# Chunked attention before a mixture of experts: 64x64 tiles of the array in place of zero blocks, and transposes moved further ahead

## The chip, the cores and the metric

The kernel runs on one core of a Trainium2 chip. The metric is the device time of one execution in microseconds (us); of the kernel before three executions were timed, with a median of 689.94 us (687.65 to 695.09). The engines are called as in the profile: PE is TensorE's matmul side and PEld its weight loads, DVE is VectorE, ACT is ScalarE, POOL is GpSimd, SP is SyncE, which here only issues DMAs.

## What is computed

Attention within chunks of 64 tokens (8 batches, 8 heads, 576 tokens, head size 64), then a mixture of 16 experts in 4 groups of 4, one expert for each of the 4608 tokens. Cut to what matters:

```python
scores = q_c @ k_c.T / 8            # a chunk of 64 tokens against itself, for each head
attn = exp(scores - max(scores))
attn = attn / (sum(attn) + 1e-9)
x = (attn @ v_c)                    # then 4608 tokens of 512 numbers
g = argmax(x @ w_group); e = argmax(x @ w_expert[g])
out = gate(g) * gate(e) * (relu(x @ w1[g, e]) @ w2[g, e])
```

All of the attention is in float32.

## The kernel before

Tokens are worked on in 36 tiles of 128 tokens, two chunks each. A tile goes through these steps, each a function with a letter, by which the order is written:

- `load_qk(u)` (Q, line 248) brings q and k of two tiles; a partition holds two neighbouring tokens of all heads. `load_v(t)` (V, line 257) brings v of a tile in four DMAs of 64 KB. Both go through SP's queue, in the order of the program. q and k have three buffers, v has `NV = 4`.
- `stage_a(t)` (a, lines 271 and 274): eight transposes on PE, into two banks of the pool `ps_t`, and four copies of 64 partitions by DVE and ACT. They give q^T and k^T for half of the heads of two tiles. k^T goes into a buffer (`kz`) in which the other head of a pair has a block of zeros.
- `stage_b(t)` (b, line 288): scores. Eight matmuls; each contracts over 128 rows (two heads) for one chunk, with 64 columns of q^T as weights and 128 columns of k^T and zeros moving. The profile has two records for each float32 matmul, so 16.
- `stage_sub` (s, lines 296 and 299, DVE), `stage_exp` (e, line 305, ACT): row maximum, difference, exponential.
- `stage_ct(t)` (c, lines 311 and 313): four transposes of the probabilities on PE, one copy by ACT.
- `stage_pv(t)` (p, line 327): weighted sums, eight matmuls of 130 columns (two heads of 64 and a column of ones, with blocks of zeros in `va`).
- `stage_norm(t)` (n, lines 341 to 352, DVE): division by the sum that the column of ones gives.
- `stage_xt(t)` (x, lines 364 and 365): four transposes for the router, one copy by ACT.

After each four tiles the router runs: logits (line 371, four matmuls of 32 columns of weights and 512 moving columns, in the four column strips of the array), a transpose back (line 384), a chain of small DVE operations (`route`, spread between others by `more`), ranks, and four indirect DMAs by POOL that put the tokens in the order of their experts.

The order on PE, DVE and ACT is written by hand: a string `HEAD` for the first tiles, a loop for tiles 8 to 34, a string `TAIL` for the end. In the loop, at step t, PE does a(t), then b(t-2), x(t-5), c(t-3), p(t-4). The first expert's weights are loaded by POOL (F0, F1, F4, F5 in `EXTRA`) and split in two parts (P0 to P7) while the attention runs. Then a loop over the experts' tokens follows, which the change leaves as it was.

Of the kernel before, what the change touches and what calls it, by code (L numbers as in the profile page):

```python
# [42 lines left out]
EXTRA = {26: "F0", 28: "F1", 29: "F2 F3 P0", 30: "P1 P2", 31: "P3", 32: "P4 P5 F4", 33: "P6 X0", 34: "P7 X1 F5"}  # L43
HEAD = ("V0 a0 Q2 a1 b0 V1 s0 a2 e0 Q3 a3 V2 b1 s1 e1 c0 a4 b2 s2 V3 c1 Q4 e2 p0 n0 a5 b3 s3 e3 V4 a6 p1 V5"
        " n1 b4 s4 c2 a7 c3 p2 n2 x0 G0 e4 b5 x1 s5 Z0 p3 e5 x2 V6 c4 Z1 Q5 n3")
TAIL = ("c32 m1 b33 m1 36 m1 s33 p31 b34 e33 V35 W1 m4 x30 m1 n31 m3 s34 m1 L0 m1 e34 L1 c33 x31 b35 17 m2"
# [14 lines left out]
def constants():  # L61
# [9 lines left out]
    # the first unit stands in the row behind the experts and goes before them  # L71
# [18 lines left out]
def moe_kernel(tc, q, k, v, w_group, w_expert, w1, w2, cst, out):  # L90
# [3 lines left out]
    with ExitStack() as ctx:  # L94
        dpool = ctx.enter_context(tc.tile_pool(name="dram", bufs=1, space=DRAM))
        wpool = ctx.enter_context(tc.tile_pool(name="wts", bufs=1))
        # the tokens of each expert in order: x, the token's number, its gate weight
# [7 lines left out]
        # rows that stand behind an expert's tokens: zeros with an out-of-range token  # L105
# [9 lines left out]
        # of the first unit: its tokens' rows, its expert, what it takes off each expert  # L115
# [23 lines left out]
        # a bank of the router's, then of the first layer's  # L139
# [14 lines left out]
        # the first unit's weights are brought in, and its w1 split, while the attention runs  # L154
        alloc_w(wpool, 0, 0, 2)

        def late2(i):
            if i not in wt[0]:
                pool, tag = ((kpool, "kz"), (vpool, "va"))[i > 3]
                m, c, n = W_PARTS[i]  # L160
                wt[0][i] = pool.tile([P, c, n], F32R, name=m + "0", tag=tag)
            return wt[0][i]
# [23 lines left out]
        def prep_static(i):  # L186
            # the first half of the columns, then the second
            i = i % 4 * 2 + i // 4
            h, l, r = (z.rearrange("p a b -> p (a b)") for z in (wt[0][0], wt[0][1], w1r[i // 4]))
            w, o = i * 512, i % 4 * 512  # L190
            nc.scalar.copy(h[:, w:w + 512], r[:, o:o + 512])
            nc.gpsimd.tensor_sub(l[:, w:w + 512], r[:, o:o + 512], h[:, w:w + 512].bitcast(F32))

        with ExitStack() as c1:
# [6 lines left out]
            ps_t = c1.enter_context(tc.tile_pool(name="pst", bufs=4, space=PSUM))  # L201
# [11 lines left out]
            # zeros where one head's part would meet the other's  # L213
            vbufs, kbufs = [], []
            for i in range(2):
                kz = kpool.tile([P, 4, 2, 2 * P], F32, name="kz%d" % i, tag="kz")
                for x in range(2):
                    (nc.gpsimd if x else nc.vector).memset(kz[64 * x:64 * x + 64, :, 1 - x, :], 0.0)
                kbufs.append(kz)
            for i in range(NV):  # L220
                va = vpool.tile([P, 2, 4, 2, HD + 1], F32, name="va%d" % i, tag="va")
                for x in range(2):
                    nc.gpsimd.memset(va[64 * x:64 * x + 64, :, :, 1 - x, :], 0.0)
                    nc.gpsimd.memset(va[64 * x:64 * x + 64, :, :, x, HD:HD + 1], 1.0)
# [13 lines left out]
            def load_qk(u):  # L238
                # a partition holds two neighbouring tokens of each head
                s = st["u", u] = {}  # L240
                both = lpool.tile([P, 2, H, P], F32, name="qk", tag="big")
                for x, nm in enumerate("qk"):
                    s[nm + "s"] = both[:, x]
                for hh in range(2) if u == 0 else (slice(None),):
                    hs = hh if u else slice(hh, H, 2)
                    for x, src in enumerate((q, k)):
                        for i, m, b, j in spans(4 * u, 4):
                            nc.sync.dma_start(
                                both[i * 32:(i + m) * 32, x, hs],
                                src[b, hs, j * CH:(j + m) * CH, :].rearrange("h (r a) d -> r h (a d)", a=2))  # L250

            def load_v(t):
                va = vbufs[t % NV]
                for c in range(2):
                    b, j = divmod(2 * t + c, NCH)
                    for x in range(2):
                        nc.sync.dma_start(
                            va[64 * x:64 * x + 64, c, :, x, 0:HD],
# [3 lines left out]
            def stage_a(t):  # L262
                u, hh = divmod(t, 2)
                s = st["u", u]
                if hh == 0:
                    s["qT"] = apool.tile([P, 4, 2 * P], F32, name="qT")
                r = slice(64 * hh, 64 * hh + 64)
                for nm, dst, eng in (("qs", s["qT"][r], nc.vector.tensor_copy if t < 2 else nc.scalar.copy), ("ks", kbufs[u % 2][r, :, hh, :], nc.vector.tensor_copy)):
                    pt = ps_t.tile([P, 4, P], F32, name="tp")
                    for i in range(4):  # L270
# [1111 lines left out]
```

## Time and profile before

| | us |
|---|---|
| median of three executions | 689.94 |
| lowest, highest | 687.65, 695.09 |
| profiled execution, span from first to last instruction | 700.9 |
| attention, to the scores of tile 32 | about 0 to 189 |
| end of the attention and the tables of the experts | about 190 to 250 |
| experts | about 250 to 688 |

The profiled execution is given by its span alone; that span is 11 us above the median of the timed ones. The page shows which engine is busy when; the chain of waits goes back from the last instruction to what each step waited for; the view of stretches gives busy time, granted clock (PEclk, 1.00 is full) and the share of the 16 DMA engines.

### The profile page before, as it was taken

To read this page: it belongs to the slowest core of one execution; us is meant where nothing else is said; L and a number is where in the kernel's file an instruction comes from. 1 tells how busy PE (TensorE), PEld (TensorE's weight loads), DVE (VectorE), ACT (ScalarE), POOL (GpSimd) and SP (SyncE) were. 2 spreads that over 40 slices of the span, in tenths; PEclk is the share of its full clock that TensorE was granted. 3 is DMA by queue.
4 is the path that set the end of the run, shared out by engine and by line. 5 is a ranking of instruction groups with operands and counts; after the bars stand their busy time and mean duration, and the time that the engine had idled before them with its cause. 6 is when DMAs were issued, how large, how long until landed. Compare 5 with 4: busy or idle time off the path is not lost.

```text
span 700.9 us, 14708 instructions
## 1 busy us (share of the span) xinstructions
PE 635.7 (91%) x4714; PEld 549.8 (78%) x4715; DVE 398.5 (57%) x738; ACT 324.1 (46%) x452; POOL 169.3 (24%) x272
## 2 busy tenths in 40 slices
PE   5989999879787879999998799999999999999991
PEld 4867777657566778898987789898999988898980
DVE  5766778747648656722649475572731868753220
ACT  5766777658544243511536355151511474551110
POOL 4002220227225222112226221222111214312110
PEclk9999999999898989999999899999999999999996
DMA  9988989999662596831357775645441757831100
GB/s 219 187 188 207 229 183 210 263 218 302 135 195 92 158 340 227 311 117 47 110 198 250 260 263 188 214 167 170 159 148 60 266 212 241 327 110 57 30 30 15
DMA packets 115946, 127.97 MB, mean 183 GB/s; under 512 B 46462, under 2 KB 83582, under 8 KB 115904
## 3 DMA queue, kind: packets, MB, share of 16 engines
q1 hardware_dynamic: 105040, 93.77, 47.2%
q0 software_dynamic: 10864, 33.64, 14.2%
q8 instruction: 26, 0.43, 0.3%
q14 instruction: 16, 0.13, 0.1%
HBM read 106.23 MB, written 21.93 MB: 183 GB/s over the span
## 4 chain that ended last, share of the span: by engine, by line
PE 75%; DMA 13%; DVE 4%; issue 3%; SPq 1%; POOL 1%; ACT 0%; another core or an unknown queue 0%; POOLq 0%; DVEq 0%; ACTq 0%
PE py L836 25%; PE ph L821 16%; DMA qk<-in_k_dram 6%; PE lgk L821 5%; PE sc L288 3%; PE o L327 3%; PE tp L271 3%; PE ph L805 3%; PE tp L364 2%; DMA xgr<-xs 2%; DMA va<-in_v_dram 2%; PE tp L311 2%; PE py L853 2%; PE pxt L721 2%; DMA out_dram<-xl,io__3010 1%
## 5 line engine op out<-in xcount | busy, mean ns | idle before, releaser
L821 PE MATMUL ph<-xt,w1h 128*128 128x256 f32 x672 | 100.3, 286 | 6.3 <-issue 6.3
L976 ACT ACTIVATE hth<-ph 128x512 fp32r<-128x512 f32 x43 | 25.7, 597 | 156.5 <-PE ph L821 124.5
L821 PEld LDWEIGHTS ph<-xt,w1h 128*128 128x128 f32 x672 | 90.8, 195 | 7.8 <-issue 6.7
L1300 POOL DMA_INDIRECT out_dram<-xl,io__3010 x37 | 44.1, 1191 | 151.6 <-DVE xl L1037 143.8
L1051 DVE TENSOR_TENSOR w2l<-w2r,w2h 128x1024 fp32r<-128x1024 f32 x60 | 69.5, 1219 | 8.5 <-ACT w2h L991 5.1
L1047 DVE TENSOR_TENSOR w1l<-w1r,w1h 128x2048 fp32r<-128x2048 f32 x28 | 63.0, 2288 | 12.7 <-ACT w1h L963 11.0
L836 PE MATMUL py<-w2h,hth 128*128 128x512 f32 x264 | 69.0, 404 | 0.0
L836 PE MATMUL py<-w2l,hth 128*128 128x512 f32 x264 | 65.8, 391 | 0.0
L836 PE MATMUL py<-w2h,htl 128*128 128x512 f32 x264 | 65.5, 390 | 0.0
L1037 DVE TENSOR_SCALAR xl<-py,io__3010 128x512 f32<-128x512 f32 x33 | 24.7, 748 | 69.2 <-PE py L836 69.2
L1070 DVE SCALAR_TENSOR_TENSOR htl<-ph,hth 128x512 fp32r<-128x512 f32 x40 | 27.4, 688 | 60.7 <-ACT hth L976 58.4
L271 PE MATMUL tp<-cs,qk 128*128 128x128 f32 x288 | 42.6, 292 | 18.8 <-DMA qk<-in_q_dram 11.7
L836 PEld LDWEIGHTS py<-w2l,hth 128*128 128x128 f32 x264 | 49.5, 188 | 10.9
L836 PEld LDWEIGHTS py<-w2h,htl 128*128 128x128 f32 x264 | 49.6, 188 | 10.8
L836 PEld LDWEIGHTS py<-w2h,hth 128*128 128x128 f32 x264 | 48.8, 192 | 10.4 <-ACT hth L1022 0.7
L271 PEld LDWEIGHTS tp<-cs,qk 128*128 128x128 f32 x288 | 33.0, 148 | 30.2 <-issue 15.6
L821 PE MATMUL ph<-xt,w1l 128*128 128x256 f32 x336 | 55.1, 287 | 0.5 <-DVE w1l L1047 0.5
L963 ACT CAST w1h<-w1r 128x2048 fp32r<-128x2048 f32 x28 | 52.1, 1902 | 4.1 <-DMA w1r<-in_moe_w_dram 2.4
L967 ACT CAST w2h<-w2r 128x2048 fp32r<-128x2048 f32 x28 | 52.3, 1925 | 0.0
L274 ACT COPY qT<-tp 64x512 f32<-64x512 f32 x70 | 44.0, 629 | 16.2 <-PE tp L271 9.4
L499 POOL DMA_INDIRECT xs<-x,pos x24 | 23.8, 990 | 100.7 <-DVE xl L352 51.0
L821 PEld LDWEIGHTS ph<-xt,w1l 128*128 128x128 f32 x336 | 47.2, 195 | 0.7 <-DVE w1l L1047 0.7
(278 smaller groups left out, 1111.8 us busy)
## 6 DMA issues: line engine op xcount, KB each, us to landing
w1r<-in_moe_w_dram SPq DMA_DIRECT2D x30, 1024.0 KB, 5.9
w2r<-in_moe_w_dram SPq DMA_DIRECT2D x30, 1024.0 KB
xgr<-xs POOLq DMA_DIRECT2D x38, 257.0 KB, 5.3
va<-in_v_dram SPq DMA_DIRECT2D x144, 64.0 KB
qk<-in_q_dram SPq DMA_DIRECT2D x11, 512.0 KB
qk<-in_k_dram SPq DMA_DIRECT2D x11, 512.0 KB
w1r<-in_moe_w_dram POOLq DMA_DIRECT2D x2, 1024.0 KB
w2r<-in_moe_w_dram POOLq DMA_DIRECT2D x2, 1024.0 KB
```

The source lines that it names most:

```text
L271: nc.tensor.transpose(pt[:, i, :], s[nm][:, 2 * i + hh, :], ident)
L274: (nc.scalar.copy if x else eng)(tv[:, :, :, x], pt[64 * x:64 * x + 64])
L821: m = pe.matmul(ph[f // 2][:, f % 2 * 256:f % 2 * 256 + 256], w_[:, c, f * P:(f + 1) * P], a_[:, c, :], start=(i == 0), stop=(i == 11))
L836: m = pe.matmul(py[j], a_[:, f, half[j]], w_(b, f), start=(i == 0), stop=(i == 23))
L963: lambda b, s, j: ac.copy(wt[b][0][:, s], w1r[j]), K1)
L967: lambda b, s, j: ac.copy(wt[b][2 + j], w2r[j]), K2)
L976: ac.activation(hth()[:, 2 * b:2 * b + 2, :], ph[b].rearrange("p (f t) -> p f t", f=2), AF.Relu).then_inc(S["Ha"], 1)
L1037: return ve.tensor_scalar(out=yb[:, j, :], in0=py[j], scalar1=io_[:, j, 1:2], scalar2=None, op0=ALU.mult)
L1047: lambda b, s, j: ve.tensor_sub(wt[b][1][:, s], w1r[j], wt[b][0][:, s].bitcast(F32)), K1, js)
L1051: m = ve.tensor_sub(wt[b][4 + 2 * j + i], w2r[j][:, 2 * i:2 * i + 2], wt[b][2 + j][:, 2 * i:2 * i + 2].bitcast(F32))
L1070: ve.scalar_tensor_tensor(out=htl()[:, 2 * b:2 * b + 2, :], in0=ph[b].rearrange("p (f t) -> p f t", f=2), scalar=0.0, in1=hth()[:, 2 * b:2 ...
L1300: gp.indirect_dma_start(out, bass.IndirectOffsetOnAxis(ap=io[:, j, 0:1].bitcast(I32), axis=0), yb[:, j, :], None, bounds_check=N - 1, oob_ ...
```

## The change

The blocks of zeros go. Each head's scores and weighted sums contract over 64 rows only, so a matmul takes a 64x64 quarter of the array; there are 16 instead of 8 in each of b and p, with half the moving columns. `sc` grows to two banks (heads in the upper and the lower rows have a bank each), so `ps_t` falls from four banks to three. q^T and k^T now hold four tiles, in four buffers; `va` has five buffers instead of four and no zeros. `stage_a(n)` is cut in two: n counts q and k apart, four transposes each. The loop is rewritten: at step t it does b(t), p(t-2), a(2t+6), c(t-1), a(2t+7), x(t-3), so q and k are transposed three tiles ahead of their scores. q and k are loaded as soon as one of their three buffers is free, and the first two tiles' q and k are loaded by tile instead of by head parity.

```diff
-NV = 4
+NV = 5
-        kpool = ctx.enter_context(tc.tile_pool(name="kz", bufs=2))
-        vpool = ctx.enter_context(tc.tile_pool(name="va", bufs=NV))
+        kpool = ctx.enter_context(tc.tile_pool(name="qkT", bufs=4))
...
-            ps_t = c1.enter_context(tc.tile_pool(name="pst", bufs=4, space=PSUM))
+            ps_t = c1.enter_context(tc.tile_pool(name="pst", bufs=3, space=PSUM))
...
+            def stage_a(n):
+                u, i = divmod(n, 8)
+                if i < 2:
+                    st["T", u, i] = kpool.tile([P, 4, 512], F32, name="kT" if i else "qT", tag="qkT")
+                dst = st["T", u, i % 2]
+                pt = ps_t.tile([P, 4, P], F32, name="tp")
+                z, x = i % 2, i // 2 % 2
...
+                for hp in range(4):
+                    nc.tensor.transpose(pt[:, hp, :], st["q", n // 4][:, z, 2 * hp + x], ident)
...
+                for a in range(2):
+                    (nc.vector.tensor_copy if z and not a else nc.scalar.copy)(to[:, a], pt[64 * a:64 * a + 64])
...
+            TILES = [(x, c, slice(64 * x, 64 * x + 64), slice(64 * c, 64 * c + 64)) for x in range(2) for c in range(2)]
             def stage_b(t):
+                sc = ps_s.tile([P, 2, 512], F32, name="sc")
                 for hp in range(4):
-                    for c in range(2):
-                        k0 = P * (t % 2) + c * CH
-                        nc.tensor.matmul(sc[c * 64:c * 64 + 64, 2 * hp:2 * hp + 2, :], lhsT=st["u", u]["qT"][:, hp, k0:k0 + CH],
-                                         rhs=kbufs[u % 2][:, hp, :, k0:k0 + CH], start=True, stop=True)
+                    for x, c, rows, cols in TILES:
+                        k0 = c0 + c * CH
+                        nc.tensor.matmul(sc[cols, x, hp * CH:hp * CH + CH], lhsT=st["T", u, 0][rows, hp, k0:k0 + CH],
+                                         rhs=st["T", u, 1][rows, hp, k0:k0 + CH], start=True, stop=True)
...
             def stage_pv(t):
-                if t in (TL - 2, TL):
-                    o = [ps_s.tile([P, 512], F32, name="sc"), bank(True, "o")]
-                else:
-                    o = ps_s.tile([P, 2, 512], F32, name="o")
+                o = ps_s.tile([P, 2, 512], F32, name="o")
                 for hp in range(4):
-                    for c in range(2):
-                        nc.tensor.matmul(o[hp // 2][c * 64:c * 64 + 64, hp % 2 * 2 * W:hp % 2 * 2 * W + 2 * W],
-                                         lhsT=pT[:, hp, c * 64:c * 64 + 64],
-                                         rhs=s["va"][:, c, hp].rearrange("p h e -> p (h e)"), start=True, stop=True)
+                    for x, c, rows, cols in TILES:
+                        nc.tensor.matmul(o[cols, x, hp * W:hp * W + W], lhsT=pT[rows, hp, cols], rhs=s["va"][rows, c, hp], start=True, stop=True)
...
-                for t in range(8, TL):
-                    stage_a(t)
-                    if t % 2 == 1 and t // 2 + 2 < NT // 2:
-                        load_qk(t // 2 + 2)
...
-                    run("b%d s%d x%d c%d e%d" % (t - 2, t - 2, t - 5, t - 3, t - 2))
-                    run("p%d n%d" % (t - 4, t - 4))
-                    load_v(t - 1)
...
+                for t in range(TL - 2):
+                    run("b%d s%d p%d n%d" % (t, t, t - 2, t - 2))
...
+                    run("a%d" % (2 * t + 6) if t else FIRST)
...
+                    run("c%d e%d" % (t - 1, t))
+                    run("a%d" % (2 * t + 7))
+                    if t % 2 == 0 and t <= 26:
+                        run("Q%d" % (t // 2 + 4))
+                    run("x%d" % (t - 3))
+                    load_v(t + 2)
```

The order on PE in one tile of the loop before (tp are the banks of the transposes; qk, pr and x are what is transposed):

```order
L271 MATMUL tp<-cs,qk 128x128 x8
L288 MATMUL sc<-kz_130,qT 64x128 x8
L364 MATMUL tp<-cs,x 128x128 x4
L311 MATMUL tp<-cs,pr 128x128 x4
L327 MATMUL o<-va_151,pT 64x130 x8
```

The same in the kernel after:

```order
L298 MATMUL sc<-kT,qT 64x64 x16
L335 MATMUL o<-va_133,pT 64x65 x16
L279 MATMUL tp<-cs,qk 128x128 x4
L323 MATMUL tp<-cs,pr 128x128 x4
L279 MATMUL tp<-cs,qk 128x128 x4
L363 MATMUL tp<-cs,x 128x128 x4
```

Scores and weighted sums now stand side by side, and the sixteen transposes of a tile behind them; before, the two stood apart, with transposes between.

The first DMAs on SP's queue before (cs are constants, qk are q and k, va is v):

```order
L101 DMA cs<-in_cst_dram 128x128
L248 DMA qk<-in_q_dram 128x4x128
L248 DMA qk<-in_k_dram 128x4x128
L248 DMA qk<-in_q_dram 128x4x128
L248 DMA qk<-in_k_dram 128x4x128
L248 DMA qk<-in_q_dram 128x8x128
L248 DMA qk<-in_k_dram 128x8x128
L626 DMA cs<-in_cst_dram 128x349
L257 DMA va_136<-in_v_dram 64x4x64 x4
```

And after, from the second q of the first pair of tiles:

```order
L249 DMA qk<-in_q_dram 128x4x64
L249 DMA qk<-in_k_dram 128x4x64
L249 DMA qk<-in_q_dram 128x8x128
L249 DMA qk<-in_k_dram 128x8x128
L249 DMA qk<-in_q_dram 32x8x128
L249 DMA qk<-in_q_dram 96x8x128
L249 DMA qk<-in_k_dram 32x8x128
L249 DMA qk<-in_k_dram 96x8x128
L258 DMA va_127<-in_v_dram 64x4x64 x4
```

q and k of three pairs of tiles stand ahead of the first v, where two pairs stood.

## Rows read from the trace of the kernel before

**Rows 1.** Stretches: us; busy us of PE, PEld, DVE, ACT, POOL; PEclk, DMA share, GB/s.

```profile
0.00:190.00 190.00, 160.50 (x1687) 127.27 (x1688) 127.76 (x367) 128.49 (x227) 46.98 (x73) 0.96 0.95 215
190.00:250.00 60.00, 47.18 (x376) 38.87 (x377) 38.80 (x118) 22.86 (x36) 21.48 (x22) 0.89 0.49 161
250.00:690.00 440.00, 428.07 (x2655) 383.63 (x2654) 231.97 (x253) 172.72 (x191) 100.83 (x178) 0.98 0.51 176
```

**Rows 2.** Chain of waits, its longest DMA pieces: start us, us, what.

```profile
40.05 8.02 DMA qk<-in_k_dram
...
86.87 10.19 DMA qk<-in_k_dram
...
158.80 6.15 DMA va<-in_v_dram
164.96 16.32 DMA qk<-in_k_dram
```

**Rows 3.** Timeline of PE, 112 to 124 us: start us, us, engine, line.

```profile
112.16 1.11 PE L327 MATMUL o<-va,pT 128*64 128x130 f32 x16
113.21 1.09 PE L271 MATMUL tp<-cs,qk 128*128 128x128 f32 x8
114.23 1.09 PE L288 MATMUL sc<-kz,qT 128*64 128x128 f32 x16
115.25 0.66 PE L364 MATMUL tp<-cs,x 128*128 128x128 f32 x4
115.75 0.60 PE L311 MATMUL tp<-cs,pr 128*128 128x128 f32 x4
116.28 1.11 PE L327 MATMUL o<-va,pT 128*64 128x130 f32 x16
...
121.59 1.07 PE L371 MATMUL lgk<-xT,wg 128*32 128x512 f32 x8
122.59 1.09 PE L271 MATMUL tp<-cs,qk 128*128 128x128 f32 x8
123.52 0.60 PE L384 MATMUL lgk<-cs,lts 128*128 128x128 f32 x4
```

**Rows 4.** Timeline, the first and a late stage b, and SP's last v.

```profile
10.18 1.09 PE L288 MATMUL sc<-kz,qT 128*64 128x128 f32 x16 [1.48 <-ACT kz L274]
...
169.25 24.57 SPq L257 DMA_DIRECT2D va<-in_v_dram  x24
...
188.89 1.09 PE L288 MATMUL sc<-kz,qT 128*64 128x128 f32 x16
```

**Rows 5.** SP's issues of one line: ns minimum/median/maximum, first and last start.

```profile
L257 SPq DMA_DIRECT2D va<-in_v_dram x144: 595/615/6269, 7.6 to 193.2; - x144
...
L248 SPq DMA_DIRECT2D qk<-in_q_dram x25: 341/602/3091, 1.4 to 164.1; - x25
L248 SPq DMA_DIRECT2D qk<-in_k_dram x25: 312/633/4194, 1.8 to 165.0; - x25
```

**Rows 6.** What SP's queue waited for: us in total, times, longest us.

```profile
SPq L257 <- PE tp L271: 14.5, 9, 5.9
...
SPq L257 <- PE o L327: 5.9, 9, 1.7
SPq L257 <- PE tp L311: 5.3, 8, 1.7
```

**Rows 7.** Stretches of 5 us, columns as in rows 1.

```profile
75.00:80.00 5.00, 5.00 (x62) 4.25 (x59) 4.08 (x10) 4.30 (x8) 0.00 (x0) 1.00 0.56 116
...
165.00:170.00 5.00, 4.95 (x57) 3.52 (x56) 4.40 (x10) 4.89 (x10) 3.03 (x4) 1.00 1.13 277
```

**Rows 8.** Timeline of the end: weighted sums and divisions of tiles 33 and 34.

```profile
205.15 0.61 PE L327 MATMUL tp<-va,pT 128*64 128x130 f32 x8
206.28 1.11 PE L327 MATMUL o<-va,pT 128*64 128x130 f32 x16
206.88 0.41 DVE L352 TENSOR_TENSOR xl<-tp,rc 128x256 f32<-128x256 f32 x1
```

More of the change, by code (lines that the diff above doesn't have):

```diff
@@ L158, in late2 @@
             if i not in wt[0]:
-                pool, tag = ((kpool, "kz"), (vpool, "va"))[i > 3]
                 m, c, n = W_PARTS[i]
-                wt[0][i] = pool.tile([P, c, n], F32R, name=m + "0", tag=tag)
+                if i < 4:
+                    wt[0][i] = kpool.tile([P, c, n], F32R, name=m + "0", tag="qkT")
+                else:
+                    j = i - i % 2
+                    both = kpool.tile([P, 2 * c, n], F32R, name=m + "0", tag="qkT")
+                    wt[0][j], wt[0][j + 1] = both[:, 0:c], both[:, c:2 * c]
             return wt[0][i]
@@ L212, in moe_kernel @@
             nc.vector.memset(wg, 0.0)
[L214 to L219, printed above, removed]
+            vbufs = []
             for i in range(NV):
[L221 to L224, printed above, removed]
+                va = cpool.tile([P, 2, 4, HD + 1], F32, name="va%d" % i)
+                (nc.gpsimd if i else nc.vector).memset(va[:, :, :, HD:HD + 1], 1.0)
                 vbufs.append(va)
@@ L257, in load_v @@
                         nc.sync.dma_start(
-                            va[64 * x:64 * x + 64, c, :, x, 0:HD],
+                            va[64 * x:64 * x + 64, c, :, 0:HD],
                             v[b].rearrange("(hp h2) s d -> h2 s hp d", h2=2)[x, j * CH:(j + 1) * CH])
                 st[t] = dict(va=va)
[L262 to L270, printed above, removed]
-                        nc.tensor.transpose(pt[:, i, :], s[nm][:, 2 * i + hh, :], ident)
-                    tv = dst.rearrange("p h (r a) -> p h r a", a=2)
-                    for x in range(2):
-                        (nc.scalar.copy if x else eng)(tv[:, :, :, x], pt[64 * x:64 * x + 64])
@@ L282, in stage_b, with bank @@
+            def bank(end):
+                return ps_t.tile([P, 4, P], F32, name="tp").rearrange("p a b -> p (a b)") if end else lgk
+            TILES = [(x, c, slice(64 * x, 64 * x + 64), slice(64 * c, 64 * c + 64)) for x in range(2) for c in range(2)]
             def stage_b(t):
-                s, u = st[t], t // 2
-                sc = bank(t >= TL - 1, "sc").rearrange("p (h k) -> p h k", h=8)
+                s, u, c0 = st[t], t // 4, t % 4 * P
+                sc = ps_s.tile([P, 2, 512], F32, name="sc")
@@ L292, in stage_sub @@
+                s["sc"] = sc[:, :, 0:4 * CH].rearrange("p x (h k) -> p x h k", h=4)
             def stage_sub(t):
@@ L349, in stage_norm @@
                 x = st["x", g][:, i, 0:D]
-                xv = x.rearrange("p (a b d) -> p a b d", a=2, d=HD)
-                for z, r, y in zip(ov, rv, [xv[:, 0], xv[:, 1]] if two else [xv]):
-                    nc.vector.tensor_tensor(out=y, in0=z[..., 0:HD], in1=r.unsqueeze(len(r.shape)).broadcast_to(list(r.shape) + [HD]),
-                                            op=ALU.mult)
+                nc.vector.tensor_tensor(out=x.rearrange("p (h x d) -> p x h d", x=2, d=HD), in0=o[..., 0:HD],
+                                        in1=rc.unsqueeze(3).broadcast_to([P, 2, 4, HD]), op=ALU.mult)
                 more()
```

90 lines of the change are left out of this document (43 added, 47 removed).

## The prediction

> **What bounds the kernel now.** I read the stretches first [rows 1]. The change touches the first 190 us only; the experts' 440 us stay as they are, and there PE is busy for 428 us. In the first 190 us PE is busy for 160.50 us, DVE for 127.76, ACT for 128.49, and the DMA engines have a share of 0.95. So two resources are close to full, PE and the transfers, and the busy times alone don't say which one sets the pace.
>
> The chain of waits goes through both. Between stretches of PE work it stands on single DMA pieces of 6 to 16 us, mostly q and k, and ends its part of the attention with 6.15 us of v and 16.32 us of k [rows 2]. The reader is to see in it that the attention, for all its busy PE, arrives several times at a tile whose data isn't there.
>
> The timeline gives PE's own demand. Where nothing is late, the weighted sums p of one tile start at 112.16 and those of the next at 116.28, 4.12 us apart: p 1.05, transposes of q and k 1.02, scores b 1.02, the x and c transposes 1.03 together [rows 3]. After each fourth tile the router adds 1.00 (line 371) and 0.53 or more around line 384, some 0.4 to 0.5 us a tile. The demand is thus about 4.6 us a tile. The pace is slower: the first b starts at 10.18 and that of tile 32 at 188.89, so 178.7 / 32 = 5.59 us a tile [rows 4]. PE waits for about 1.0 us of each.
>
> SP's queue explains these waits. It carries q, k and v in program order; when it waits for a buffer, all behind it waits. Its waits for buffers that PE frees sum to 14.5 + 5.9 + 5.3 = 25.7 us [rows 6]. The transfers also come unevenly: from 75 to 80 us PE is busy throughout and the DMA share is 0.56 at 116 GB/s, from 165 to 170 it is 1.13 at 277 GB/s [rows 7]. So PE and the transfers hold each other up in turn, each being late by what the other made late before. 5.59 is more than either asks for alone.
>
> **The change part by part.**
>
> *Scores and weighted sums.* b goes from 16 records of 128 columns to 32 of 64, p from 16 of 130 to 32 of 65. Record-columns stay at 2048 (2080), but four tiles of the array can take them where two did. The trace has no 64x64 tile. Line 371 is the nearest row: four column strips, 8 records of 512 columns, so 4096 record-columns in 1.00 us, twice b's rate of 2048 in 1.02 with two strips [rows 3]. At that rate b and p take 0.50 us each, and the saving is 0.52 + 0.55 = 1.07 us a tile. The ends: if tiles of upper and lower rows don't overlap, 1.02 as now and nothing saved; if the 32 records went one behind the other at today's 1.02 / 16 = 64 ns, 2.05 us, a loss of 1.0 a stage. I take 0.50, because line 371 shows four tiles side by side at full rate and b shows that 16 short ones are no slower per column than long ones. I add 0.1 us for the tile shape, which changes twice a tile instead of four times. PE's demand falls from 4.6 to about 3.45 us a tile.
>
> Line 371's eight records overlap within those 1.00 us, so whatever a record costs by itself was hidden there by 512 columns [rows 3]. The Trainium skill, in "TensorEngine Tiling (Array Packing)", section "Instruction Overhead", says that every matmul costs about 60 cycles here and that a tiling factor shouldn't be taken from a dimension that is already small. No run here shows that price on 64 columns; by it, as an estimate at 2.4 GHz, 32 records are 0.8 us a stage instead of 0.50. It speaks against this change, which has just doubled the records and halved the columns; its result is weighed with rival 1.
>
> *The copies.* DVE and ACT have 127.76 and 128.49 us for 33 tiles, 3.87 and 3.89 us a tile [rows 1]; the number of copied elements and the shapes stay. They take 3.9 us a tile, under 4.67 below, so at the forecast's pace they remain cover. `ps_t` has three banks instead of four, and the sixteen transposes now come in one row, four stages into three banks: PE may wait for a copy there. From nothing to 0.3 us a tile; I take it as part of the 0.3 of waits below. The memsets of the zero blocks are POOL's, beside other work: nothing.
>
> *The queue.* Bytes and packet shapes stay. What the queue needs when nothing blocks it is bounded from below by its issues: 144 x 0.615 + 25 x 0.602 + 25 x 0.633 = 119.5 us [rows 5], 119.5 / 36 = 3.3 us a tile. From above: its last v ends at 169.25 + 24.57 = 193.8 us [rows 4]; less the 25.7 us in which it waited for PE that is 168, or 4.67 us a tile; in this the transfers' own slowness is still contained. A check from bytes: 215 GB/s for 190 us are 40.9 MB [rows 1]; at 277 GB/s, the highest rate in the rows [rows 7], they need 147 us, 4.1 a tile. I take 4.67, since it is what this queue did under these very transfers.
>
> *The lookahead.* Q of a pair is issued about five tiles before its use where it was three, v has a fifth buffer, and q and k are transposed three tiles ahead of b. SP's sequence still goes past v in order. A v issue now waits for p of a tile five back instead of four. This takes away part of the waits and adds none that I can name, except at the start: q and k of a third pair stand ahead of the first v, four DMAs of some 0.6 us each [rows 5], about 2 us of SP, while the first p comes only two tiles after the first b. From nothing to 2 us, once; I take nothing.
>
> *The end.* `o` is a single buffer of two banks, so p of tile 34 waits for the division of tile 33. Today p34 starts at 206.28, before that division's last step at 206.88 with 0.41 us [rows 8]: it would start about 1 us later, at 207.3, and finish half a microsecond sooner. Plus 0.7 us with what follows for p35; at worst 2 us.
>
> *The sum.* PE's demand of 3.45 and the copies' 3.9 fall under the queue's 4.67. The present pace lies 5.59 - 4.67 = 0.92 over it, because demand and queue interfere. With PE more than 1 us under the queue, and more lookahead, I leave a third, 0.3 us. That gives 4.95 us a tile, and 32 x (5.59 - 4.95) = 20.5 us less; with 0.7 at the end, 20 less. Of the profiled execution, span 700.9, that makes 681. The timed median is 11 us under that span. If these 11 us are spread over the whole, the saving stays 20 and the time is 670. If all of them are transfer waits of the attention, its timed pace is (178.7 - 11) / 32 = 5.24, and only 32 x 0.29 = 9 are to be had: 681. The nearer reading is the first, as nothing in the rows puts them in one stretch. **Forecast: 670 us**; its own range is 657 (no waits over 4.67: 29.4 less, with up to 4 us more from a queue nearer to 4.5) to 683.
>
> **The rivals.**
>
> 1. *The quarters give half or nothing.* If each record has a price that short ones don't hide, or if upper and lower rows take turns, b and p end between 0.8 and 1.02 us. At 0.8 PE's demand is 4.6 - 0.47 = 4.1, still close to the queue, and the two interfere nearly as now; then about half of the saving, 10 us: 680. At 1.02 the lookahead alone remains, perhaps 5 us: 685. For it: no row shows row halves side by side. Against: pairs of b already overlap. The rule of the Trainium skill named above would give the 680. Chance 0.13.
>
> 2. *The transfers are full already.* The share is 0.95 over the 190 us [rows 1]; if that is a limit, 0.05 x 190 = 9.5 us are all there is, and half of it is likelier: 685. For it: the chain stands on DMA pieces [rows 2], and 165 to 170 us shows a share above 1 while k is late. Against: 0.56 while PE was the one busy [rows 7], and 277 GB/s against a mean of 215. Chance 0.15.
>
> 3. *Slower.* The 32 records of a stage go one behind the other at 64 ns, 2.05 us a stage: PE's demand is 4.6 + 2.06 = 6.66, above all else, and 32 x (6.66 - 5.59) = 34 more: 724. It decides from the point where a stage takes more than about 1.5 us, since two such stages bring the demand to 5.55, the present pace. For it: all 64x64 tiles that share rows or columns might be kept apart. Against: b's two strips, which share their rows, run together [rows 3]. Chance 0.11.
>
> 4. *Freed as far as the copies.* If the DMA share is only backlog and the rate of 277 GB/s can be held, the copy engines set the pace: 3.9 + 0.3 = 4.2 us, 32 x 1.39 = 44 less: 646. For it: the 4.1 from bytes. Against: the weights of the first expert and the indirect DMAs lie in the same time. Chance 0.09.
>
> **How the numbers follow.** The forecast has 0.52. About 1%, 7 us, is what a measurement of this kernel can tell from no change, so faster means under 683 and slower over 697. Faster: all but 0.03 of the forecast's 0.52, rival 4 with 0.09, half of rival 1 and a third of rival 2, together 0.49 + 0.09 + 0.07 + 0.05 = 0.70. Slower: rival 3 with 0.11 and 0.01 of an end that costs more than I see. The rest, 0.18, is no change. The range leaves out rival 3 and most of rival 4 and reaches over the first two with some room: 650 to 690.
>
> **What would show it.** Right, if b and p are groups of about 0.5 us each, b of tile 32 starts at about 169 instead of 188.89, SP's waits for PE fall well below 25.7 us, the DMA share of 0 to 170 us rises above 1.0, and the experts' stretch keeps its 438 us. The PE step is wrong if b or p takes 0.8 us or more; the queue step, if the pace is above 5.3 with short stages (the transfers were full) or below 4.5 (4.67 was still backpressure). The covers are wrong if the transposes wait for their three banks, a `tp` wait on DVE or ACT of more than 0.3 us a tile. The experts would make all of it wrong if their stretch moved by more than 3 us, since nothing in the sum speaks of them.

## The result and the profile after

| | us |
|---|---|
| changed kernel, median of 18 executions | 699.04 (694.21 to 703.34) |
| kernel before, median of 18 executions beside them | 693.93 (687.45 to 699.01) |
| ratio | 1.0086, 95% interval 1.006 to 1.0112 |
| profiled execution after, span | 701.3 |

The changed kernel is slower by 0.9%, with an interval clear of no change, where 670 us were forecast and a range of 650 to 690. The ratio leaves out the slow executions of the kernel before, so it is not the quotient of the two medians, 1.0074.

The stretches of the changed kernel, to be read beside [rows 1]:

```profile
0.00:190.00 190.00, 142.43 (x2679) 117.00 (x2681) 118.72 (x340) 125.53 (x216) 37.81 (x56) 0.90 0.90 209
190.00:250.00 60.00, 49.99 (x533) 41.96 (x532) 41.14 (x136) 24.93 (x42) 20.41 (x21) 0.83 0.44 138
250.00:690.00 440.00, 426.90 (x2658) 383.14 (x2656) 235.60 (x258) 175.22 (x192) 94.81 (x181) 0.99 0.51 182
```

PE works 18 us less in the first 190 us, and the rest of those 190 us is idle. The DMA share and GB/s are what they were, a little lower. The granted clock fell from 0.96 to 0.90.

The timeline of PE after, a tile without waits and the one behind it (start us, us, line; what PE waited for in brackets), beside [rows 3]:

```profile
119.68 0.69 PE L298 MATMUL sc<-kT,qT 64*64 64x64 f32 x32
120.20 0.65 PE L335 MATMUL o<-va,pT 64*64 64x65 f32 x32
120.78 0.66 PE L279 MATMUL tp<-cs,qk 128*128 128x128 f32 x4
121.27 0.60 PE L323 MATMUL tp<-cs,pr 128*128 128x128 f32 x4
121.71 0.60 PE L279 MATMUL tp<-cs,qk 128*128 128x128 f32 x4
124.31 1.05 PE L363 MATMUL tp<-cs,x 128*128 128x128 f32 x4 [2.00 <-ACT qT L283]
125.29 1.13 PE L298 MATMUL sc<-kT,qT 64*64 64x64 f32 x32
```

b takes 0.52 us from its start to that of p, and p 0.58 to the next: the quarter tiles do run side by side, at the rate of line 371. Then x's transposes wait 2.00 us for ACT's copy of q^T, and after the wait the same stages take about twice as long (b 1.13 us as shown, 0.69 before): the clock is at its half level for a few us.

What PE waited for between 10 and 197 us (us in total, times, longest us):

```profile
PE tp L363 <- ACT qT L283: 19.2, 24, 3.1
PE o L335 <- DMA va<-in_v_dram: 12.1, 8, 3.4
```

And SP up to 200 us:

```profile
SPq L258 <- DMA qk<-in_k_dram: 8.3, 11, 1.9
SPq L249 <- DMA va<-in_v_dram: 7.4, 7, 2.0
SPq L258 <- DMA va<-in_v_dram: 5.3, 3, 2.4
SPq L249 <- PE tp L279: 3.8, 4, 1.4
SPq L258 <- PE tp L323: 2.8, 2, 2.3
SPq L258 <- PE sc L298: 2.0, 2, 1.4
```

[rows 6] has the three longest of SP's waits for PE. The same view of the kernel before goes on:

```profile
SPq L248 <- DMA va<-in_v_dram: 4.2, 6, 1.0
SPq L257 <- PE tp L364: 4.0, 4, 2.5
SPq L257 <- PE sc L288: 3.7, 4, 1.6
SPq L257 <- DMA qk<-in_k_dram: 3.2, 6, 0.8
```

Summed over all rows, SP's waits for PE fell from 35 to 12 us: the lookahead did what the change says. Yet its v come no sooner, because the rest of SP's time grew. Its waits for q, k and v to land went from 8 to 21 us. Its issues of q, k and v went from 129 us for 194 to 146 us for 198, if the waits for buffers that their records hold are taken off. (A record does hold its wait: the longest issue of v, 6.27 us in [rows 5], starts at 129.27 us, its buffer comes free at 135.16, and this is the wait of 5.9 us in [rows 6].)

The longest pieces of the chain of waits between 20 and 190 us are still transfers and SP's issues, now mostly of v, beside [rows 2]:

```profile
25.55 7.27 DMA va<-in_v_dram
...
46.95 5.88 DMA qk<-in_k_dram
56.73 2.62 SPq L258
...
68.05 8.52 DMA va<-in_v_dram
78.50 2.12 SPq L258
82.08 6.83 DMA va<-in_v_dram
141.61 12.60 DMA va<-in_v_dram
```

**Where the attention lost.** Counted by the starts of b in the timeline, tile 5 begins at 31.27 us in the kernel before and at 38.22 after; tile 33 at 188.89 and 196.39. Both kernels need 5.63 and 5.65 us a tile between these, and the last p starts at 207.91 and 215.06. So the 7 us were lost by tile 5, and nothing was won or lost behind it. (The prediction calls the b at 188.89 that of tile 32. It is the 34th, tile 33, so the pace from the first b is 178.7 / 33 = 5.42.) That the two profiled spans, 700.9 and 701.3 us, hardly differ does not speak against this: behind that b the execution before took 512.0 us and the one after 504.9. The place of the loss is in the timeline of the changed kernel's PE:

```profile
28.88 0.69 PE L298 MATMUL sc<-kT,qT 64*64 64x64 f32 x32
32.96 1.72 PE L335 MATMUL o<-va,pT 64*64 64x65 f32 x32 [3.38 <-DMA va<-in_v_dram]
34.61 1.11 PE L279 MATMUL tp<-cs,qk 128*128 128x128 f32 x4
...
38.22 1.07 PE L298 MATMUL sc<-kT,qT 64*64 64x64 f32 x32
```

p of tile 2 waits 3.38 us for v, which stands on SP behind q and k of two further pairs of tiles. From 32.96 on every stage runs at the half clock, p in 1.72 us instead of 0.65, to 39.1 us.

### The profile page after: what moved, and what is told of

It reads as the page before. It is cut to its first block, busy times and chain, and to the rows that moved or that the text cites. A ratio compares the mean times of both kernels' runs of the same rounds, so it can differ in the third digit from the quotient of the medians.

```text
span 701.3 us, 16822 instructions
## 1 busy us (share of the span) xinstructions
PE 619.3 (88%) x5866; PEld 542.1 (77%) x5867; DVE 395.5 (56%) x731; ACT 325.7 (46%) x450; POOL 153.0 (22%) x258
## 4 chain that ended last, share of the span: by engine, by line
PE 68%; DMA 9%; DVE 6%; ACT 6%; SPq 5%; issue 4%; POOL 0%; DVEq 0%; POOLq 0%; ACTq 0%
PE py L831 24%; PE ph L816 16%; PE lgk L816 5%; DMA va<-in_v_dram 5%; PE ph L800 4%; ACT qT L283 2%; SPq L258 2%; PE tp L279 2%; SPq L249 2%; DMA qk<-in_k_dram 2%; PE tp L363 2%; PE o L335 2%; PE py L848 2%; PE sc L298 2%; PE pxt L716 2%
## 5 line engine op out<-in xcount | busy, mean ns | idle before, releaser
L971 ACT ACTIVATE hth<-ph 128x512 fp32r<-128x512 f32 x43 | 25.7, 598 | 157.4 <-PE ph L816 154.8
L1295 POOL DMA_INDIRECT out_dram<-xl,io__3559 x37 | 39.2, 1059 | 157.4 <-DVE xl L1032 142.9
L283 ACT COPY qT<-tp 64x512 f32<-64x512 f32 x68 | 41.8, 615 | 28.9 <-PE tp L279 28.1
L279 PE MATMUL tp<-cs,qk 128*128 128x128 f32 x272 | 50.3, 317 | 2.9 <-ACT pT L325 1.6
L498 POOL DMA_INDIRECT xs<-x,pos x24 | 23.7, 987 | 121.5 <-DMA va<-in_v_dram 74.4
L335 PE MATMUL o<-va,pT 64*64 64x65 f32 x1152 | 33.0, 243 | 18.8 <-DMA va<-in_v_dram 12.1
## 6 DMA issues: line engine op xcount, KB each, us to landing
qk<-in_q_dram SPq DMA_DIRECT2D x11, 512.0 KB
qk<-in_k_dram SPq DMA_DIRECT2D x11, 512.0 KB, 6.4
```

What stands on the lines that cost most here:

```text
L279: nc.tensor.transpose(pt[:, hp, :], st["q", n // 4][:, z, 2 * hp + x], ident)
L283: (nc.vector.tensor_copy if z and not a else nc.scalar.copy)(to[:, a], pt[64 * a:64 * a + 64])
L335: nc.tensor.matmul(o[cols, x, hp * W:hp * W + W], lhsT=pT[rows, hp, cols], rhs=s["va"][rows, c, hp], start=True, stop=True)
L1295: gp.indirect_dma_start(out, bass.IndirectOffsetOnAxis(ap=io[:, j, 0:1].bitcast(I32), axis=0), yb[:, j, :], None, bounds_check=N - 1, oob_ ...
```

## Experiments

The measure for the attention is the start of b of tile 5 and of tile 33, and the pace between. "few v" loads v for the first four or five tiles alone.

Each start is read from one profiled execution. e17 is the kernel of e9 once more and e18 that of e8, and their b33 lie 5.9 and 3.8 us from the first, their b5 1.4 and 2.3 us; smaller differences in the table tell nothing by themselves. e1 to e4, e5 to e8, e9 to e12, e13 to e16, and e17 with e18 ran on five different chips. Each ratio is to the kernel before on the same chip; the starts have no such neighbour.

| kernel | b5 us | b33 us | us a tile | ratio to before (95%) |
|---|---|---|---|---|
| before | 31.27 | 188.89 | 5.63 | 1 |
| changed | 38.22 | 196.39 | 5.65 | 1.0086 (1.006 to 1.0112) |
| e1, changed, exp moved (no effect on its place) | 37.39 | 192.95 | 5.56 | 1.0117 (1.0041 to 1.0193) |
| e2, tiles in the old order | 30.00 | 189.71 | 5.70 | 1.0017 (0.9977 to 1.0056) |
| e3, changed, b and p twice | 37.12 | 223.26 | 6.65 | 1.0506 (1.0416 to 1.0595) |
| e5, changed, exp behind copies | 37.45 | 196.78 | 5.69 | 1.0119 (1.0047 to 1.019) |
| e8, tiles, old order, half of v by POOL | 34.63 | 180.81 | 5.22 | 0.9881 (0.9806 to 0.9955) |
| e9, before, half of v by POOL | 36.37 | 183.80 | 5.27 | 0.9889 (0.9816 to 0.9962) |
| e10, changed, half of v by POOL | 40.25 | 196.54 | 5.58 | 1.0027 (0.9981 to 1.0073) |
| e11, e10 and e5 together | 42.10 | 195.30 | 5.47 | 1.0023 (0.9981 to 1.0065) |
| e17, the kernel of e9 again | 34.96 | 177.86 | 5.10 | 0.9921 (0.9886 to 0.9956) |
| e18, the kernel of e8 again | 32.38 | 177.03 | 5.17 | 0.9883 (0.9829 to 0.9937) |
| e12, p in tiles, half of v by POOL | 32.55 | 179.38 | 5.24 | 0.9969 (0.9924 to 1.0014) |
| e4, changed, few v | 37.05 | 178.21 | 5.04 | |
| e6, tiles in the old order, few v | 29.83 | 169.08 | 4.97 | |
| e7, before, few v | 31.60 | 169.19 | 4.91 | |
| e13, e6 without the scores' exp | 31.96 | 156.21 | 4.44 | |
| e15, p in tiles, four banks, few v | 30.75 | 158.64 | 4.57 | |
| e16, e6 with a's transposes twice | 32.12 | 171.10 | 4.96 | |

### The tiles without the new order: e2

To the kernel before:

```diff
-                sc = bank(t >= TL - 1, "sc").rearrange("p (h k) -> p h k", h=8)
+                sc = ps_s.tile([P, 2, 512], F32, name="sc")
...
+                    for x, c, rows, cols in TILES:
+                        nc.tensor.matmul(sc[cols, x, hp * CH:hp * CH + CH], lhsT=st["u", u]["qT"][rows, hp, k0:k0 + CH],
+                                         rhs=kbufs[u % 2][rows, hp, x, k0:k0 + CH], start=True, stop=True)
...
-            ps_t = c1.enter_context(tc.tile_pool(name="pst", bufs=4, space=PSUM))
+            ps_t = c1.enter_context(tc.tile_pool(name="pst", bufs=3, space=PSUM))
```

> Edit to the kernel before: scores and weighted sums as four 64x64 tiles, with the old order of stages, loads, buffers and zero blocks left in memory (not read). Scores need two banks, so the transposes have three banks instead of four, as in the changed kernel. Theory 1 (the new order is what loses, because its four transposes stand in one row behind three banks): faster than the kernel before by 5 to 15 us, and the stretch to b of tile 33 shorter than 188.9 us. Theory 1b (three banks alone lose it, in any order): as slow as the changed kernel, about 699. Theory 2 (transfers set the pace): within 3 us of the kernel before.

Theory 2 held: 1.0017, no difference. PE's busy time fell by as much as in the changed kernel, and waits took its place. The stretch, columns as in [rows 1]:

```profile
0.00:190.00 190.00, 142.56 (x2711) 113.27 (x2715) 127.12 (x367) 127.47 (x227) 47.17 (x73) 0.92 0.90 215
```

What PE waited for from 10 to 190 us:

```profile
PE tp L271 <- DMA qk<-in_k_dram: 15.4, 10, 3.2
PE o L327 <- DMA va<-in_v_dram: 9.4, 6, 2.5
PE tp L271 <- DMA qk<-in_q_dram: 6.0, 5, 3.0
```

These 30.8 us stand where 13 us of waits for q, k and v stood between 10 and 197 us before. SP in turn waits for PE for 44 us, over all rows, against 35 before. The clock is at its half level for 31 of the first 190 us, where it was for 17. So the quarter tiles, alone, neither gain nor lose.

### Twice the work of b and p: e3

To the changed kernel, in `stage_b` and `stage_pv`:

```diff
-                for hp in range(4):
+                for hp in (0, 1, 2, 3) * 2:
```

> Edit to the changed kernel: every matmul of b and p is issued twice, the second time over the same result, which adds 2 x 0.52 us of PE a tile, 37 us in all, so that PE's demand is that of the kernel before again. Theory 1 (waits for copies and banks hold PE, about 44 us of idle PE in 10 to 197 us): the added work falls partly into waits and keeps the clock up, 5 to 15 us slower than the changed kernel. Theory 2 (transfers): at most 5 us slower. Theory 3 (PE is the bound): 30 us or more slower.

By the numbers theory 3 nearly held: by the ratios the run is some 29 us over the changed kernel. The trace takes that back. PE stands still with nothing that the profile shows as its cause. Its timeline at 51 us, and what it waited for up to 215 us:

```profile
50.97 0.53 PE L335 MATMUL o<-va,pT 64*64 64x65 f32 x24
54.43 1.36 PE L335 MATMUL o<-va,pT 64*64 64x65 f32 x40 [2.93 <-issue]
```

```profile
PE o L335 <- issue: 17.4, 10, 4.3
...
PE sc L298 <- issue: 5.2, 5, 2.7
PE tp L279 <- issue: 2.6, 1, 2.6
```

These stops are told of in the last section; they cost about as much as the run lost, so e3 does not show that PE's arithmetic bounds the changed kernel.

### v left out: e4, e6, e7

```diff
-                for c in range(2):
+                for c in range(2 if t < NV else 0):
```

> Edit to the changed kernel: v is loaded for the first five tiles alone, and later tiles use these buffers again, so 31 of 36 tiles' v transfers, 124 DMAs of 64 KB, are left out. The values differ and the experts get other tokens, so only the attention's stretch, to b of tile 33 (196.39 us in the changed kernel), is to be compared. Theory 1 (copies, banks and ACT's queue): the 12 us of waits for v go, and the half clock behind them, but the 19 us for ACT's copies stay: b of tile 33 at 175 to 185. Theory 2 (transfers set the pace): a third of the bytes of q, k and v goes, b of tile 33 at 160 or earlier.

> Edit: the 64x64 tiles in the old order, three banks (as in e2), with v loaded for the first four tiles alone, so that 128 DMAs of 64 KB are left out; the values differ, and only the attention's stretch to b of tile 33 is to be compared (e2: 189.71). Theory 2 (in the old order the quarter tiles' gain went into waits for q, k and v): with a third of the transfers gone, b of tile 33 at 150 to 160 us, 4.3 to 4.6 us a tile. Theory 1b (three banks or copies set the pace): 175 or later.

> Edit: the kernel before with v loaded for the first four tiles alone, 128 DMAs of 64 KB left out; the values differ, and only the attention's stretch to b of tile 33 is to be compared (before: 188.89). Theory 2: PE's demand of 4.6 us a tile sets the pace, b of tile 33 at 165 to 172, so that the quarter tiles show their gain beside e6 (10 us or more) only where transfers are out of the way. Theory 1b: as e6 within 5 us.

Without most of v's transfers all three kernels go 0.6 to 0.7 us a tile faster: transfers are part of the bound in each. e4 came where theory 1 put it, at 178.21, and its waits for ACT's q^T copy rose to 23.7 us. e7 came where theory 2 put it, but e6, at 169.08 beside 169.19, fits neither of its theories: with 1 us less of PE work a tile, the tiles still give nothing. In e7 PE is busy for 171.89 of the first 190 us, so there its own work is close to the bound; in e6 it isn't (stretch of e6):

```profile
0.00:190.00 190.00, 157.24 (x3020) 124.51 (x3022) 139.25 (x406) 135.76 (x243) 51.03 (x77) 0.93 0.71 190
```

### What takes the slack once v is out of the way: e13 to e16

e13 and e14, then e16:

```diff
-                nc.scalar.activation(pr, pr, AF.Exp, scale=0.125)
...
-                    for i in range(4):
+                    for i in (0, 1, 2, 3) * 2:
                         nc.tensor.transpose(pt[:, i, :], s[nm][:, 2 * i + hh, :], ident)
```

e15 is the kernel before with e2's edit of `stage_pv` alone, which needs no further bank; v for four tiles alone.

> Edit to e6 (quarter tiles in the old order, v loaded for four tiles alone): the exponential of the scores on ACT (0.63 us a tile) is left out as well, so the values differ and only b of tile 33 counts (e6: 169.08). Theory A (ACT and DVE set the pace once PE has slack): 10 to 20 us earlier, 150 to 159. Theory B (the lost bank) and theory C (PE's stops and its half clock): within 4 us of 169.

> Control for e13: the kernel before with v loaded for four tiles alone (e7, b of tile 33 at 169.19) and the scores' exponential left out. PE was busy for 172 of the first 190 us in e7, so all theories expect little, within 5 us of 169; if it comes as early as e13, ACT held both kernels.

> Edit to e7: quarter tiles in the weighted sums alone, with four banks for the transposes; v for four tiles alone. PE's demand is between e7's and e6's. Theory B (three banks cost e6 its gain): b of tile 33 at 152 to 163, earlier than both e6 and e7. Theory A and C: 165 to 170.

> Edit to e6: every transpose of q and k is issued twice over the same result, which adds 1.02 us of PE a tile, as much as the quarter tiles save, with half as many instructions as doubling b and p takes. If PE truly has slack in e6 (theory A or B), b of tile 33 stays within 4 us of 169.08. Theory C (PE, with its stops and half clock, is still what sets the pace): 15 us or more later, or, if the work keeps the clock up, less half clock than e6's 30.7 us and the same end.

b of tile 33, in the order e6, e13, e15, e16, each from its own timeline:

```profile
169.08 1.13 PE L290 MATMUL sc<-kz,qT 64*64 64x64 f32 x32
```

```profile
156.21 0.69 PE L290 MATMUL sc<-kz,qT 64*64 64x64 f32 x32
```

```profile
158.64 1.09 PE L290 MATMUL sc<-kz,qT 128*64 128x128 f32 x16
```

```profile
171.10 0.69 PE L290 MATMUL sc<-kz,qT 64*64 64x64 f32 x32
```

e16 gives PE 1.02 us a tile more, 34 us by tile 33, and loses 2. Some of this is the clock: at half level for 25 of the first 190 us in e6, it is so for 3 in e16, which is worth at most half of 22 us. The other 20 us or so, give or take the 6 us by which two executions differ, are slack that PE has in e6; 7 us of it are stops of which the last section tells. The stretch of e16:

```profile
0.00:190.00 190.00, 172.74 (x3316) 147.44 (x3318) 142.88 (x408) 139.46 (x246) 51.04 (x77) 0.99 0.71 191
```

e13 takes 0.63 us a tile from ACT, some 21 us, and wins 12.9 us: with v out of the way, ACT's work is in the chain that sets the pace. e15 saves half as much PE work as e6, keeps the fourth bank and wins 10.4 us. The bank that the scores' tiles cost may be the reason, but this is not shown: e15 also has fewer short matmuls, 0.6 us of those stops where e6 has 7.3, and 11 us of half clock in the first 190 where e6 has 25, and no run takes the bank away alone. e14 gave no control: each of its matmuls took 2.4 times as long from the first tile on (mean 675 ns for line 271's transposes, 279 in e7 with the same q and k), while DVE's and ACT's instructions kept their times. Its trace has no record of the clock, and why it was so stayed open.

### SP's queue: e8, e9, e10, e11, e12, and e17, e18

```diff
-                        nc.sync.dma_start(
+                        (nc.gpsimd if x else nc.sync).dma_start(
```

> Edit to e2's kernel: of v's four DMAs a tile two are issued by POOL instead of SP; the bytes and packets stay. Theory 2a (what is full is SP's queue, 10 issues of 0.6 us or more for two tiles, in order, with its waits for buffers): q and k come earlier, and the kernel is 5 to 15 us faster than e2, so faster than both. Theory 2b (the 16 DMA engines are what is full): within 3 us of e2. It can also lose where POOL stands waiting for the router's positions with v behind it: then waits for v grow by more than those for q and k fall.

> Edit to the kernel before: two of v's four DMAs a tile issued by POOL instead of SP, as in e8, with the zero blocks kept. With the kernel before, e2 and e8 this makes a table of two by two. Theory 2a (SP's queue and PE share the bound: the kernel before waits 13 us for q and k, and its PE demand is 4.6 us a tile): some 3 to 6 us faster than before, less than the 7 to 8 us by which e8 is faster than e2, since PE sets the pace soon after. If it is as fast as e8 (within 3 us of 687), the quarter tiles give nothing even then. If it is within 2 us of before, the gain of e8 is the tiles', freed by the queue.

> Edit to the changed kernel: two of v's four DMAs a tile issued by POOL. Theory 1 (its order has a chain over ACT and DVE of some 5 us a tile, as the run with few v showed with b of tile 33 at 178): 3 to 6 us faster than the changed kernel, about 694, not faster than the kernel before. Theory 2 (transfers alone set its pace): 10 us or more faster, about 687, as e8.

> Edit to the kernel before: the 64x64 tiles in the weighted sums alone, which need no further bank, so the transposes keep four; scores with their zero blocks; two of v's four DMAs by POOL. If three banks cost e8 something, this is as fast as e8 (about 687) or faster although it saves only 0.52 us of PE a tile; if PE's work counts and the banks don't, it lies half way between e9 and e8.

The bytes are the same, and the old order goes 0.36 (e9) to 0.48 us a tile (e8) faster. So the 16 engines were not at a limit of their own at a share of 0.96: the first 160 us of the kernel before, of e9 and of e17, columns as in [rows 1]:

```profile
0.00:160.00 160.00, 136.55 (x1446) 108.13 (x1448) 107.88 (x317) 107.09 (x189) 30.96 (x57) 0.97 0.96 213
0.00:160.00 160.00, 136.76 (x1449) 109.33 (x1451) 108.13 (x318) 107.24 (x189) 67.08 (x114) 0.97 1.06 215
0.00:160.00 160.00, 141.93 (x1517) 114.33 (x1518) 113.73 (x327) 113.33 (x200) 74.38 (x123) 0.96 1.09 229
```

The packets are not the same, though e8's expectation takes them to be. Issued by SP, v goes in packets of 256 B, issued by POOL in packets of 4 KB. The rows of SP's queue on the pages of the kernel before and of e9 (packets, MB, share of the 16 engines):

```profile
q1 hardware_dynamic: 105040, 93.77, 47.2%
q1 hardware_dynamic: 85456, 89.04, 46.0%
```

So it is the way through SP's one queue that costs time here. These runs do not part what of it: SP's issues, v's waits for buffers that stand ahead of q and k, or the small packets. e8 and e9 are faster than both kernels, and they don't differ. Both once more, side by side:

> The kernel of e9 (the kernel before with two of v's four DMAs by POOL) in five rounds: if its gain is real, 0.985 to 0.993 of the kernel before.

> The kernel of e8 (64x64 tiles in the old order, two of v's four DMAs by POOL) beside e17. If the transfers still set the pace with half of v on POOL, the tiles give nothing: within 0.004 of e17. If PE was the bound there, 0.01 or more below e17.

e17: 0.9921 (0.9886 to 0.9956), e18: 0.9883 (0.9829 to 0.9937). The difference of 0.0038 lies well within the intervals, and the medians of all twelve executions, 685.22 and 686.98, lie the other way round. What helps is to take v off SP's queue, and the tiles add nothing that can be measured. e12, with half of the tiles, is at 0.9969, between the kernel before and e9, and is told apart from neither. Its b of tile 33 lies between those of e8 and e9 and those of their repeats, and it took 515 us behind it (e9: 506), so it does not answer its question on the banks.

For the new order e10 settles little. By the ratios it is 0.6% faster than the changed kernel, with intervals that overlap, and its pace, 5.58, hardly moved. Its waits for v are down from 12.1 us to 0.5, but stops for which the profile shows no cause, 0.9 us in the changed kernel, have taken their place (PE, 10 to 197 us):

```profile
PE tp L363 <- ACT qT L283: 19.1, 23, 2.1
PE o L335 <- issue: 13.4, 19, 2.3
```

### The router's exponential in the new order: e1, e5, e11

In `route`, e5 (in e1 it went one routing step less far):

```diff
-                nc.scalar.activation(ex, ls, AF.Exp)
...
                     if i == 0:
-                        V.tensor_reduce(out=sm, in_=ex, axis=AX.X, op=ALU.add)
+                        nc.scalar.activation(ex, ls, AF.Exp)
```

> Edit to the changed kernel: the router's exponential on ACT (line 412) is issued two routing steps later, so that ACT doesn't stand there waiting for DVE's routing chain with the copies of q^T and of the probabilities queued behind it. Nothing else moves. Theory 1 (ACT's queue and the three banks hold PE: x's transposes wait 19.2 us in 24 waits for ACT's q^T copy, some 2.0 us at each router, and the clock is at its half level right after): the 2.0 us waits shrink to about 0.5, 7 x 1.5 = 10 us, and with them several of the 3.4 us stretches at half clock go, up to 8 us more; 10 to 18 us faster than the changed kernel, about 681 to 689. Theory 2 (transfers set the pace): the waits move to v and q/k, within 3 us of the changed kernel. Theory 3 (PE's own work is still the bound): no change.

> Edit to the changed kernel: the router's exponential now stands behind the q^T copies in ACT's order (in the first try it had kept its place between x^T's copy and q^T's, line 422 still ran at 122.28 us, right before q^T's copies at 122.57), and the sum over it is taken two steps later on DVE. Theory 1 (in the new order a chain from b over DVE and ACT back to x's transposes sets the pace, longest where the router's exponential stands ahead of q^T's copies): the 2.0 us waits of x go, 4 tiles take about 18.5 us instead of 20 to 20.8, b of tile 33 about 10 us earlier than 196.39, where transfers allow. Theory 2 (transfers set the pace): waits for v and q/k take the place, no more than 4 us.

> Edit to the changed kernel: both the router's exponential behind the q^T copies (e5) and two of v's four DMAs by POOL (e10). Theory 1: with v out of the way the move of the exponential now shows, 5 us or more faster than e10, below 690. If it is within 3 us of e10, the exponential is not what holds the new order, with or without v.

e1 was a miss: it didn't change ACT's order. e5 did, and the waits of x's transposes fell from 19.2 to 11.1 us, but the time did not; the same stops without a cause in the profile came instead (PE, 10 to 197 us):

```profile
PE tp L363 <- ACT qT L283: 11.1, 22, 1.5
PE o L335 <- issue: 11.0, 18, 2.6
PE o L335 <- DMA va<-in_v_dram: 7.9, 7, 3.4
```

So e5 alone leaves theory 1 open. With half of v on POOL, e11 and e10 ran on one chip, both with such stops (17 and 15 us), and differ by 0.0004. By what was set down for e11, the exponential's place is not what holds the new order. The waits for the copies of q^T are there in all its runs, but what would relieve them was not found.

## Why the prediction was wrong

- **Scores and weighted sums.** Right in size: 0.50 us each were taken, 0.52 and 0.58 were measured, and PE's busy time fell by 18 us in the first 190. Rival 1's price of 0.8 us a stage isn't borne out: 32 records of 64 columns took 0.52 us, half of what 16 of 128 columns took, so a column costs the same as before. The 0.1 us for the tile shape is shown by no run.
- **The queue: the step that failed.** 4.67 us a tile came from SP's span less 25.7 us of waits for PE, as if the rest of SP's time would stay as it was. It did not. With all waits for PE, 35 us, the same working gives (193.8 - 35) / 36 = 4.4 us for the kernel before; for the changed kernel it gives (198.6 - 12) / 36 = 5.2. The waits for PE went, and waits for landings (8 to 21 us) and longer issues (129 to 146 us) took their place, and the last v starts at 198.0 us instead of 193.2. The pace was 5.65 us a tile with stages of 0.5 us, which is the sign that the prediction itself set for a wrong queue step. What makes the queue slow was not parted; half of v by POOL brings the old order to 5.1 to 5.3.
- **The interference.** 0.92 us a tile was read as two demands holding each other up, two thirds of it to be had. (With the count of tiles put right it is 0.75, the saving 33 x (5.42 - 4.95) = 15.5 us, and the forecast 675.) When PE's share alone went, in e2, PE's waits for transfers rose from 13 to 31 us and SP's waits for PE from 35 to 44: nothing was to be had.
- **The copies.** They were to be cover, with up to 0.3 us a tile of waits for a bank. By the prediction's own sign this failed: x's transposes wait 19.2 us for ACT's copy of q^T, 0.6 us a tile. Whether that costs time with the transfers as they are is not shown, since in e5, where these waits fell to 11.1 us, the stops came. With v out of the way the pace is 4.4 to 5.0 us a tile (e6, e13, e15), above the 3.9 of the copy engines' busy time. The Trainium skill says in "TensorEngine Tiling (Array Packing)", section "PSUM Bottleneck", that the copies out of the banks may become the bound once tiling has made TensorE four times as fast. Here b and p became twice as fast; e13 and e16 point the same way, with 12.9 us won and 2 lost, though what e13 takes from ACT is not itself a copy.
- **The start.** Up to 2 us were allowed and nothing was taken for q and k of a third pair ahead of v. In the trace tile 2's v also stands behind q and k of two further pairs. It cost 7 us by tile 5: with v on SP alone, b of tile 5 starts at 37 to 38 us in every run of the new order and at 30 to 32 in the old. The loss lies in waits for v and in half clock behind them, and by the traces it is the whole of the loss. That an order of loads with v further ahead would give it back was not tried.
- **The end.** 0.7 us were added. p of tile 34 does start 1.54 us late, behind DVE, but from b of tile 33 to the last p it is 18.7 us against 19.0: nothing.
- **The rivals.** The nearest was the second, transfers full, at 685 with 0.15. It was right that transfers take back what PE gives up, but its limit, a share of 0.95 of the 16 engines, is not one: e9 and e17 went to 1.06 and 1.09. The slower case was put on matmuls one behind the other, which did not happen; the loss came from the start, which had no rival of its own.

## What to carry to other kernels

A queue's waits for another engine must not be subtracted from its span to get what it needs alone: here two thirds of them went and the rest of its time grew by at least as much. Nor is the sum of its issues a bound, since the record of an issue can hold a wait; look inside the long ones. Before work is taken from the busiest engine, give it some more, work that waits for nothing: where that costs little (e16), taking it away wins little. Where an edit changes the order of loads, walk through the first five tiles by hand: the 7 us lost there were still lost at tile 33. And run one kernel twice before a difference between two profiles is believed: here that alone moved tile 33 by 4 to 6 us.

## What the runs showed of the hardware

- In e3 PE stops 15 times in the first 215 us for 0.5 to 4.5 us, some 29 us in all, and counted in the trace these stops lie, but for a few records, whole multiples of 256 PE instructions (weight loads and matmuls) apart: 256, 512, 256, 256, 1280, 256 and so on. A 16 KB instruction packet stands in the trace at most of them. The number of these packets is 26 before, 40 after and 58 in e3. The Trainium skill, "Runtime: NRT & Kernel Launch", section "Instruction fetch mechanics", tells of blocks of 16 KiB with 256 instructions, at a cost that is mostly hidden. The block agrees; the cost does not, in a kernel where 64 short instructions run in 0.5 us while the DMA engines carry q, k and v. That PE waits for these packets is the likely reading; no run varied it. The row of the page of e3 (packets, MB, share of the 16 engines):

```profile
q8 instruction: 58, 0.95, 0.6%
```

- In several executions with quarter tiles PE also stops, mostly inside p or b and for about 0.6 us at a time, with nothing in the profile that it waits for. From 10 to 197 us these stops come to 12.9 us in e5, 7.3 in e6, 15.4 in e8, 14.8 in e10 and 16.9 in e11, and 7 to 11 us of them lie beside POOL's indirect DMAs of the router. The kernel alone does not set them: e18, the kernel of e8 on another chip, has 4.5 us, the changed kernel 0.9, e2 2.2. With zero blocks e7 has 0.2, e9 2.6 and e17 none. It wasn't tested what sets them off.
- The same 64 KB of v stand in the trace as 256 packets of 256 B where SP issues them, and as packets of 4 KB where POOL does (e8, e9, e10, e17).
- A wait of 2 to 3 us costs PE more than itself: in the changed kernel the clock goes to its half level for 3.4 us or more behind each of them. In the first 215 us the half clock lasts 20 us before and 50 us after.
